# A float64 weight decoder without its sign step: Prelu with slope 2**32 in place of Copy

## The chip, the cores and the metric

The kernel runs on one core of one Trainium2 chip. The metric is device time in microseconds (us); where several executions were timed, the median is given. Engines are named as the profile names them: PE is TensorE's matrix products and PEld its weight loads, DVE is VectorE, ACT is ScalarE, POOL is GpSimd, SP is SyncE, which issues most of the DMAs.

## The reference

Linear attention over 2304 tokens is followed by two feed-forward layers (512 to 2048 to 512), the first with an ELU, the second with mish. The four weight matrices are float64. Cut to what matters:

```python
q_s = softmax(q, axis=-1)            # per head; 4 batches, 8 heads, 576 tokens, 64 wide
k_s = softmax(k, axis=2)             # over the tokens
x = einsum(q_s, einsum(k_s, v))      # 2304 tokens x 512
h = x @ w1_in                        # float64 weights
x = where(h > 0, h, exp(min(h, 0)) - 1) @ w1_out
h = x @ w2_in
return (h * tanh(log1p(exp(h)))) @ w2_out
```

## The kernel before

**The weights.** They come as the bits of their float64 values, two 32-bit words each, and are taken in pieces: one f-tile, 128 hidden units, of `w_in` or of `w_out`, 128 partitions x 512 values. There are 64 pieces, 16 f-tiles of two matrices in two layers. A piece is loaded by SP (`load_piece`), and then decoded to float32 in place:

- `rebias` (ACT, L148) rescales the high words, read as float32, by 2**-112;
- `decode_low` (DVE, L152) shifts the low words right by 29;
- `decode_sign` (DVE, L159) takes the top bit of the high word into the low word;
- `decode_join` (DVE, L166) shifts the high word left by 3 and ors the low word into it.

`piece_hi` (ACT, L186) rounds the value to its 12 leading bits, and `piece_lo` (POOL, L192) subtracts that from the value: every float32 product runs as three passes, hi*lo + lo*hi + hi*hi. Of the second layer's pieces both parts go to DRAM and come back later.

**The tokens.** The first layer takes its tokens in five blocks of four and three tiles of 128 by turns, the second in six blocks of three. In a block, a slot is one f-tile: 12 matmuls of `mm_h` (PE, L397) into one of two PSUM banks, the ELU in `elu_exp` and `elu_neg` (ACT, L405 and L409) and `elu_join` (DVE, L413, which reads the bank and so frees it), a split into hi and lo (ACT L426, DVE L430), and two slots later 12 matmuls of `mm_y` (PE, L443). Beside the products of a block run the attention steps of the next: the key chain (maximum L243, exponential L250, transposes, kv products) and the query chain (`q_max` on DVE, `q_less` L323, `q_exp` L329 on ACT, `q_sum` on DVE, `q_norm` L338, the transposes L348, `q_x` L362). In block 0 `q_less` and `q_norm` run on POOL.

**What sets the order.** Every engine takes its instructions in program order, and the program is written out by hand. Until the pipeline is full, the table `FIRST` gives the order of the steps: `1i0` is `decode_low` of piece 0 of `w_in`, `2i0` its `decode_sign`, `3i0` its `decode_join`, `b`, `p` and `l` are `rebias`, `piece_hi` and `piece_lo`; `mh` and `mr` are the two halves of a slot's `mm_h`, `ej` its `elu_join`, `gl` its low part, `my` its `mm_y`. The pieces i0 to i6 and o0 to o4 go by the table. From slot 5 of block 0 a loop does: in each slot two pieces in the rest of block 0 (`rebias` at the end of the slot ahead, `decode` behind `split_hi`, `split_piece` behind `elu_neg`), and of the second layer one piece every two slots in blocks 1 to 4.

Of the kernel before, what the change touches and what calls it, by code (L numbers as in the profile page):

```python
# [11 lines left out]
AF = mybir.ActivationFunctionType  # L12
# [5 lines left out]
EPS = 1e-9  # L18
# tanh(log1p(u)) = n / (n + 2) with n = u (u + 2). From u = 2**14 on it rounds to 1 in float32,
# as the reference's tanh does beyond its bound of 20, so u is held there.  # L20
U_MAX = 16384.0


# What comes before the pipeline is full, in the order in which the engines take it. A step's name
# tells what it does (see where they are made), and ends with the number of its pair of heads, tile
# of tokens, f-tile or piece of the weights; x0 and on are what runs beside the first slots.
FIRST = """
    km0 km1 qm0 km2 ke0 ql0 kt0 ke1 kr0 qe0 kt1 km3 ke2 kt2 qm1 kr1 ke3 ql1 ks0 ku1 qs0 kt3
    ks1 qn0 kr3 1i0 qt0 bi0 ks3 ku0 qe1 inv ku3 2i0 qm2 kv0 qs1 kr2 qm3 qn1 kv1 ku2 kv3 ql2
    kz0 ql3 ks2 qt1 qu0 kv2 kz1 qe2 qe3 3i0 kz3 kz2 qs2 qs3 qx0 qu1 1i1 pi0 qn3 qx1 bi1 bi2  # L30
    xh0 qn2 2i1 li0 xl0 qt3 qt2 xh1 qu2 1i2 xl1 qu3 qx2 xh2 2i2 3i1 1o0 qx3 xl2 xh3 pi1 bi3
    mh0 bo0 li1 xl3 mr0 1i3 mh1 mr1 3i2 bo1 2o0 pi2 ee0 en0 li2 x0 bi4 3o0 x1 ej0 2i3 1i4
    1o1 po0 2o1 ld0 gh0 bo2 3i3 ee1 mh2 gl0 mr2 2i4 lo0 en1 3i4 x2 pi3 li3 1o2 ee2 ej1 2o2
    my0 x3 en2 pi4 ld1 3o2 ej2 li4 x4 gh1 x5 mh3 gh2 x6 bo3 x7 mr3 3o1 1i5 mh4 gl1 bi5 1i6
    mr4 1o3 2i5 po1 2o3 bi6 3o3 po2 lo1 gl2 x8 ee3 x9 po3 x10 x11 2i6 ee4 3i5 my1 1o4 bo4
    en3 2o4 3i6 x12 x13 lo2 x14 pi5 3o4 ej3 lo3 en4 x15 li5 x16 ej4 gh3 my2 ld3 pi6 mh5 ld2
    mr5 po4 li6 x17 ld4 lo4 gl3 x18
""".split()
# [3 lines left out]
def attention_elu_mish(  # L42
# [10 lines left out]
):  # L53
    """The weights come as the bits of their float64 values, [..., 2] words each, low word first.

    float32 products run as three float32r passes: each operand is split exactly into
    hi (its 12 leading bits) and lo (the rest), and hi*lo + lo*hi + hi*hi accumulate in PSUM."""
    nc = tc.nc
# [8 lines left out]
    FG = NF // NG  # L67
    # The first MoE takes its tokens in blocks of four and three tiles of 128 by turns (what lies
    # on chip alternates between two buffers), the second in blocks of three.
    TILES = (4, 3, 4, 3, 4)  # L70
# [7 lines left out]
    NB = NT // TB  # L78
    # the second MoE's blocks, by tiles: the first two find theirs on chip, the others in DRAM
    back = [t for t in range(at0[NA - 2])] + [at0[NA - 1] + TPB]  # L80
# [36 lines left out]

# [1 line left out]
    # A piece is what one f-tile takes: w_in's columns, or w_out's rows, of 128 hidden units.  # L119
    raw = {}  # L120
# [22 lines left out]
    def rebias(*keys):  # L143
        # The scale moves the exponent's bias (1023 to 127, where it lies 20 bits up); three bits
        # further up it is float32's, and the sign and three more bits of the fraction go beside it.
        for key in keys:
            high = raw[key].bitcast(F32)[:, :, 1]
            nc.scalar.activation(out=high, in_=high, func=AF.Copy, scale=2.0 ** -112)  # L148

    def decode_low(*keys):  # L150
        for t in (raw[key] for key in keys):
            nc.vector.tensor_scalar(  # L152
                out=t[:, :, 0], in0=t[:, :, 0], scalar1=29, scalar2=None,
                op0=ALU.logical_shift_right,
            )

    def decode_sign(*keys):
        for t in (raw[key] for key in keys):
            nc.vector.scalar_tensor_tensor(  # L159
                out=t[:, :, 0], in0=t[:, :, 1], scalar=0x80000000, in1=t[:, :, 0],  # L160
                op0=ALU.bitwise_and, op1=ALU.bitwise_or,
            )
# [8 lines left out]
    def decode(*keys):  # L171
        decode_low(*keys)
        decode_sign(*keys)
        decode_join(*keys)
# [31 lines left out]

# [1 line left out]
    ap = att.enter_context(tc.tile_pool(name="att", bufs=2))  # L208
# [81 lines left out]
    def k_kv(b, hp, ps=None):  # L290
        e, vv = en_t.pop((b, hp)), v_t.pop((b, hp))
        if ps is None:
            ps = att_psum()
        for c in range(NC):
            n = min(P, S - c * P)
            # a head's half of the array's columns is all that it needs, and both work at once
            for a in (0, D):
                nc.tensor.matmul(  # L298
                    out=ps[a:a + D, a:a + D], lhsT=e[0:n, c, a:a + D], rhs=vv[0:n, c, a:a + D],
                    start=(c == 0), stop=(c == NC - 1),  # L300
                )
        kv_t[b, hp] = ps
# [80 lines left out]

# [1 line left out]
    h_t, e_t, gh_t, gl_t, y_t = {}, {}, {}, {}, {}  # L385
# [62 lines left out]
    def end_y(j):  # L448
        for e in range(KD):
            ps = y_t[e][:, 0:TILES[j] * P]  # L450
            hi, lo = xh[j][:, e, :], xl[j][:, e, :]
            nc.scalar.activation(out=hi, in_=ps, func=AF.Copy)
            nc.vector.tensor_tensor(out=lo, in0=ps, in1=hi.bitcast(F32), op=ALU.subtract)
        # tiles that lie side by side on either side go together
        runs = []
        for t in range(at0[j], at0[j] + TILES[j]):
            if t in back:
                b, o = divmod(back.index(t), TPB)
                if runs and runs[-1][0] == b and o:
                    runs[-1][3] += 1  # L460
                else:
                    runs.append([b, o, t - at0[j], 1])
        for b, o, t, n in runs:
            for d, x in zip(x2_d[b], (xh[j], xl[j])):
                nc.gpsimd.dma_start(
                    out=d[:, :, o * P:(o + n) * P], in_=x[:, :, t * P:(t + n) * P]
                )

    # mish(h) = h n / (n + 2) with u = e**h, n = u (u + 2). The reciprocal is e**-ln(n + 2), which
    # one step of Newton's method makes exact to float32. What two f-tiles need goes turn by turn.  # L470
    def mish(f, old, older):
# [66 lines left out]
    x2 = {}  # L538
# [5 lines left out]

    # the second batch's values are loaded early, where the second block's tokens will lie
    for n, t in enumerate(("xhb", "xlb")):
        t = xpool.tile([P, KD * TB], F32, tag=t, name="early_x")
        for hp in (2 * n, 2 * n + 1):
            a = hp % 2 * NC * P
            v_t[1, hp] = t[:, a:a + NC * P].rearrange("p (c e) -> p c e", e=P)  # L550
# [1 line left out]
    beside = {}  # L552
# [9 lines left out]
    def kv_chain(j, f, b):  # L562
        for hp in range(NHP):
            # the slots in which a load is emitted lie behind what frees its buffer
            s = f + 2 * hp
# [25 lines left out]

    # the first layer's pieces come in the first block's slots, two in each
    turns = {-1: [("i", 0, 0), ("i", 0, 1)]}
# [8 lines left out]
    for j in range(NA - 1):  # L602
        if j + 1 < B:
            kv_chain(j, 0, j + 1)
        for o in range(TILES[j + 1]):
            q_chain(j, (8 if TILES[j + 1] == TPB else 6) + 2 * o, at0[j + 1] + o)
    # the second MoE's are decoded over the other blocks, and wait in DRAM
    for n in range(NF):
# [10 lines left out]
    with tc.manual_schedule():  # L619
        nc.scalar.preload_act_table_set("natural_log_exp_and_others")  # L620
        two = const.tile([P, 1], F32, name="two")
        nc.vector.memset(two, 2.0)
        # what comes first is loaded at once, where later weights will lie
        tags = ("wih", "wil", "woh", "wol")
# [54 lines left out]
        for hp in range(2, NHP):  # L679
            load_v(1, hp, v_t[1, hp])  # L680
        # the array's clock rises only once the array has been busy
        warm = ps_h.tile([P, 512], F32, tag="h", name="t")
# [15 lines left out]
        def step(name, fn, *a):  # L698
            first[name] = lambda: fn(*a)
# [22 lines left out]
        for key in [key for f in range(-1, AHEAD) for key in turns[f]]:  # L722
            n = f"{key[0]}{key[2]}"
            step("b" + n, rebias, key)
            step("1" + n, decode_low, key)
            step("2" + n, decode_sign, key)
            step("3" + n, decode_join, key)
            step("p" + n, piece_hi, *key)
            step("l" + n, piece_lo, *key)
        # the first products take their tokens by halves  # L730
        half = slice(0, 2 * P), slice(2 * P, 4 * P)
# [55 lines left out]
        for s in range(len(slots) + LAG2):  # L787
            if s < len(slots):
                p, f = slots[s]
                # two banks that the second block's outputs take lend room while the pipe fills  # L790
                mm_h(1, *x2[p], f, TB, pool=(ps_a, "a") if p == 0 and f in (2, 3) else None)
# [47 lines left out]
```

## Time and profile before

| | |
|---|---|
| median of 3 runs | 886.6 us (885.91 to 886.83) |
| profiled execution, its span from first to last instruction | 885.3 us |
| what lies around the span, as the difference of the two | 1.3 us |
| PE, DVE, ACT, POOL busy | 866.6, 643.9, 471.9, 168.1 us |
| last sign step of VectorE | in block 4 of the first layer, before 470 us |

The time of the profiled execution beside its span is not given by itself; the median of the runs stands for it. Busy shares are averages over stages that have different limits. The stages here are the attention of the first block (to 27 us), the fill of the pipeline (to 59 us), the rest of block 0 (to 125.5 us), blocks 1 to 4 of the first layer (to 470 us), and the second layer. A PE that is busy in a stage sets its pace; where PE is idle, what it waited for is looked up. The clock column is the granted TensorE clock as a share of full speed.

### The profile page before, as it was taken

The page shows a single profiled execution, that of the slowest core. Times are in us where ns is not written, and L with a number is a line of the kernel's source. Part 1 is how long each engine was busy: PE and PEld are TensorE (multiplying, and loading weights), DVE is VectorE, ACT ScalarE, POOL GpSimd, SP SyncE. Part 2 cuts the span into 40 slices and gives each one's busy share as a digit, 9 for nine tenths or more (in the row PEclk, how much of TensorE's full clock was granted, in tenths as well). Part 3 has the DMA queues.
Part 4 walks back from the last instruction along what each step waited for, and adds up shares of the span by engine and source line. Part 5 has one row for each costly group of instructions (what it writes and reads, how often), then busy time and mean ns, then how long its engine had stood idle before and what let it go on. Part 6 is the DMA issues. An engine that isn't in the chain of part 4 may idle for free.

```text
span 885.3 us, 12486 instructions
## 1 busy us (share of the span) xinstructions
PE 866.6 (98%) x4644; PEld 769.7 (87%) x4644; DVE 643.9 (73%) x1210; ACT 471.9 (53%) x935; POOL 168.1 (19%) x183
## 2 busy tenths in 40 slices
PE   8889999999999999999999999999999999999998
PEld 5878779999888899998888899999999999999996
DVE  7999976776555557845444977778877877877875
ACT  6768756655655455554444544444544544544443
POOL 2346653322321233223333000000000000000000
PEclk7999999999999999999999999999999999999999
DMA  9763364654634355536977302102002102000100
GB/s 299 235 195 128 118 211 117 197 176 141 170 107 147 96 162 152 163 96 191 284 243 224 129 1 72 37 0 72 37 1 72 37 1 72 36 1 1 37 1 36
DMA packets 60381, 99.37 MB, mean 112 GB/s; under 512 B 4001, under 2 KB 38817, under 8 KB 58273
## 3 DMA queue, kind: packets, MB, share of 16 engines
q1 hardware_dynamic: 38720, 52.44, 19.4%
q0 software_dynamic: 21600, 46.14, 17.0%
q8 instruction: 36, 0.59, 0.3%
q14 instruction: 25, 0.20, 0.1%
HBM read 70.78 MB, written 27.79 MB: 111 GB/s over the span
## 4 chain that ended last, share of the span: by engine, by line
PE 85%; DVE 9%; issue 3%; ACT 1%; DMA 1%; POOL 0%; SPq 0%; POOLq 0%; DVEq 0%; ACTq 0%
PE h L397 40%; PE y L443 19%; PE y L523 15%; PE a L523 7%; DVE early L159 2%; DVE early L166 2%; PE a L362 1%; DVE early L152 1%; DVE gl L430 1%; DVE e L413 1%; PE a L348 1%; PE a L298 1%; PE t L298 1%; DMA early<-in_kT_dram 1%; DVE raw L159 0%
## 5 line engine op out<-in xcount | busy, mean ns | idle before, releaser
L397 PE MATMUL h<-xha,wil 128*128 128x384 f32 (+2 forms) x408 | 144.6, 354 | 4.1 <-DVE ks L254 2.8
L397 PE MATMUL h<-xha,wih 128*128 128x384 f32 (+2 forms) x408 | 144.5, 354 | 0.0
L397 PE MATMUL h<-xla,wih 128*128 128x384 f32 (+2 forms) x408 | 144.2, 353 | 0.0
L495 ACT ACTIVATE r<-n,two 128x384 f32<-128x384 f32 x96 | 59.5, 619 | 132.1 <-DVE n L491 132.1
L443 PE MATMUL y<-gh,wol 128*128 128x512 f32 (+1 forms) x320 | 122.8, 384 | 0.0
L443 PE MATMUL y<-gl,woh 128*128 128x512 f32 (+1 forms) x320 | 118.3, 370 | 0.5 <-DVE gl L430 0.5
L443 PE MATMUL y<-gh,woh 128*128 128x512 f32 (+1 forms) x320 | 118.4, 370 | 0.0
L413 DVE SCALAR_TENSOR_TENSOR e<-h,e 128x512 f32<-128x512 f32 (+1 forms) x80 | 50.8, 636 | 89.1 <-ACT e L409 89.0
L397 PE MATMUL h<-xhb,wih 128*128 128x384 f32 x320 | 107.6, 336 | 0.0
L397 PE MATMUL h<-xhb,wil 128*128 128x384 f32 x320 | 107.4, 336 | 0.0
L397 PE MATMUL h<-xlb,wih 128*128 128x384 f32 x320 | 107.3, 335 | 0.0
L405 ACT ACTIVATE e<-h 128x512 f32<-128x512 f32 (+1 forms) x80 | 44.3, 554 | 108.6 <-PE h L397 108.6
L192 POOL TENSOR_TENSOR lo<-raw,hi 128x512 fp32r<-128x512 f32 x32 | 45.9, 1435 | 240.0 <-ACT hi L186 147.6
L397 PEld LDWEIGHTS h<-xha,wil 128*128 128x128 f32 x408 | 77.3, 190 | 13.9 <-issue 5.0
L474 ACT ACTIVATE u<-h 128x384 f32<-128x384 f32 x96 | 47.1, 491 | 74.7 <-PE h L397 74.7
L397 PEld LDWEIGHTS h<-xla,wih 128*128 128x128 f32 x408 | 77.3, 189 | 8.6
L484 DVE TENSOR_SCALAR u<-u 128x384 f32<-128x384 f32 x96 | 35.3, 368 | 66.5 <-ACT u L474 66.5
L397 PEld LDWEIGHTS h<-xha,wih 128*128 128x128 f32 x408 | 77.3, 189 | 6.5
L523 PE MATMUL y<-woh,gl 128*128 128x512 f32 x192 | 76.1, 397 | 0.0
L523 PE MATMUL y<-woh,gh 128*128 128x512 f32 x192 | 76.0, 396 | 0.0
L523 PE MATMUL y<-wol,gh 128*128 128x512 f32 x192 | 74.7, 389 | 0.0
L430 DVE TENSOR_TENSOR gl<-e,gh 128x512 fp32r<-128x512 f32 (+1 forms) x80 | 51.7, 646 | 29.3 <-ACT gh L426 29.3
(139 smaller groups left out, 1820.0 us busy)
## 6 DMA issues: line engine op xcount, KB each, us to landing
raw<-in_moe_w_out_dram SPq DMA_DIRECT2D x23, 512.0 KB, 4.3
raw<-in_moe_w_in_dram SPq DMA_DIRECT2D x21, 512.0 KB, 5.1
early<-in_moe_w_in_dram SPq DMA_DIRECT2D x11, 512.0 KB, 6.0
early<-in_moe_w_out_dram SPq DMA_DIRECT2D x9, 512.0 KB, 6.2
out_dram<-o SPq DMA_DIRECT2D x18, 256.0 KB, 2.3
q<-in_q_dram SPq DMA_DIRECT2D x16, 256.0 KB, 5.1
w2ih<-hi POOLq DMA_DIRECT2D x16, 256.0 KB, 3.9
w2il<-lo POOLq DMA_DIRECT2D x16, 256.0 KB, 4.9
```

Of the source, the lines that this page charges most:

```text
L159: nc.vector.scalar_tensor_tensor(out=t[:, :, 0], in0=t[:, :, 1], scalar=0x80000000, in1=t[:, :, 0], op0=ALU.bitwise_and, op1=ALU.bitwise_or,)
L166: nc.vector.scalar_tensor_tensor(out=t[:, :, 1], in0=t[:, :, 1], scalar=3, in1=t[:, :, 0], op0=ALU.logical_shift_left, op1=ALU.bitwise_or,)
L192: nc.gpsimd.tensor_tensor(out=lo, in0=z, in1=hi.bitcast(F32), op=ALU.subtract)
L397: nc.tensor.matmul(out=h_t[f][:, c], lhsT=w[:, i, k * P:(k + 1) * P], rhs=x[:, k, c], start=(n == 0), stop=(n == 3 * KD - 1),)
L405: nc.scalar.activation(out=e, in_=h_t[f], func=AF.Exp)
L413: nc.vector.scalar_tensor_tensor(out=e, in0=h_t[f], scalar=0.0, in1=e, op0=ALU.max, op1=ALU.subtract)
L430: nc.vector.tensor_tensor(out=gl_t[f], in0=h_t.pop(f), in1=gh_t[f].bitcast(F32), op=ALU.subtract)
L443: nc.tensor.matmul(out=y_t[e][:, 0:gh.shape[1]], lhsT=w[:, i, e * P:(e + 1) * P], rhs=x, start=(f == 0 and n == 0), stop=(f == NF - 1 and ...
L474: nc.scalar.activation(out=u, in_=h_t[f], func=AF.Exp)
L484: nc.vector.tensor_scalar(out=u, in0=u, scalar1=U_MAX, scalar2=None, op0=ALU.min)
L495: nc.scalar.activation(out=r, in_=n, func=AF.Ln, bias=two)
L523: nc.tensor.matmul(out=y_t[p, t], lhsT=x[:, c], rhs=w[:, i, :], start=(f == 0 and n == 0), stop=(f == NF - 1 and n == 2),)
```

## The change

`rebias` uses the function Prelu in place of Copy: with the scale of 2**-112 and a slope of 2**32 on the negative side. A negative word then has an exponent that is 32 higher, and the bit for 32 in it is the one that the shift by 3 in `decode_join` brings to the place of the sign. `decode_sign` goes, and with it its steps in `FIRST`; the join, which was step 3, is now step 2. The other steps stand in the order that they had.

```diff
         for key in keys:
             high = raw[key].bitcast(F32)[:, :, 1]
-            nc.scalar.activation(out=high, in_=high, func=AF.Copy, scale=2.0 ** -112)
+            nc.scalar.activation(
+                out=high, in_=high, func=AF.Prelu, scale=2.0 ** -112, alpha=2.0 ** 32
+            )
...
-    def decode_sign(*keys):
-        for t in (raw[key] for key in keys):
-            nc.vector.scalar_tensor_tensor(
-                out=t[:, :, 0], in0=t[:, :, 1], scalar=0x80000000, in1=t[:, :, 0],
-                op0=ALU.bitwise_and, op1=ALU.bitwise_or,
-            )
-
...
     def decode(*keys):
         decode_low(*keys)
-        decode_sign(*keys)
         decode_join(*keys)
...
-            step("2" + n, decode_sign, key)
-            step("3" + n, decode_join, key)
+            step("2" + n, decode_join, key)
```

Of the table one line shows the pattern:

```diff
-    mr4 1o3 2i5 po1 2o3 bi6 3o3 po2 lo1 gl2 x8 ee3 x9 po3 x10 x11 2i6 ee4 3i5 my1 1o4 bo4
+    mr4 1o3 po1 bi6 2o3 po2 lo1 gl2 x8 ee3 x9 po3 x10 x11 ee4 2i5 my1 1o4 bo4
```

The lines below `decode_sign` move up by five in the changed kernel: `decode_low` is L155 there, `decode_join` L162, `elu_join` L408, the low part L425.

On VectorE at the end of the fill, from the low part of f-tile 1 to the ELU join of f-tile 3 (`early_134` and `early_135` hold raw pieces), there stands before:

```order
L430 TENSOR_TENSOR gl_596<-e_473,gh_546 128x512
L152 TENSOR_SCALAR early_135<-early_135 128x512
L152 TENSOR_SCALAR early_134<-early_134 128x512
L159 SCALAR_TENSOR_TENSOR early_134<-early_134 128x512 x2
L166 SCALAR_TENSOR_TENSOR early_134<-early_134 128x512
L430 TENSOR_TENSOR gl_620<-e_514,gh_562 128x512
L159 SCALAR_TENSOR_TENSOR early_135<-early_135 128x512
L166 SCALAR_TENSOR_TENSOR early_134<-early_134 128x512
L152 TENSOR_SCALAR early_135<-early_135 128x512
L159 SCALAR_TENSOR_TENSOR early_135<-early_135 128x512
L166 SCALAR_TENSOR_TENSOR early_135<-early_135 128x512 x2
L413 SCALAR_TENSOR_TENSOR e_624<-h_549,e_624 128x512
```

And in the changed kernel, at the same place on VectorE:

```order
L425 TENSOR_TENSOR gl_588<-e_467,gh_538 128x512
L155 TENSOR_SCALAR early_135<-early_135 128x512
L155 TENSOR_SCALAR early_134<-early_134 128x512
L162 SCALAR_TENSOR_TENSOR early_134<-early_134 128x512
L425 TENSOR_TENSOR gl_610<-e_507,gh_554 128x512
L162 SCALAR_TENSOR_TENSOR early_134<-early_134 128x512
L155 TENSOR_SCALAR early_135<-early_135 128x512
L162 SCALAR_TENSOR_TENSOR early_135<-early_135 128x512 x2
L408 SCALAR_TENSOR_TENSOR e_614<-h_541,e_614 128x512
```

The four sign steps (L159) between the two are gone; what is left stands in the order of before.

On VectorE in the later slots of block 0, two slots with their query chain (`qs` and `qm` are its sums and maxima), there stands before:

```order
L152 TENSOR_SCALAR raw<-raw 128x512 x2
L159 SCALAR_TENSOR_TENSOR raw<-raw 128x512 x2
L166 SCALAR_TENSOR_TENSOR raw<-raw 128x512 x2
L430 TENSOR_TENSOR gl<-e,gh 128x512
L413 SCALAR_TENSOR_TENSOR e<-h,e 128x512
L382 TENSOR_TENSOR xlb<-a,xhb 128x4x128
L333 TENSOR_REDUCE qs<-q 128x8
```

And in the changed kernel:

```order
L155 TENSOR_SCALAR raw<-raw 128x512 x2
L162 SCALAR_TENSOR_TENSOR raw<-raw 128x512 x2
L425 TENSOR_TENSOR gl<-e,gh 128x512
L408 SCALAR_TENSOR_TENSOR e<-h,e 128x512
L377 TENSOR_TENSOR xlb<-a,xhb 128x4x128
L328 TENSOR_REDUCE qs<-q 128x8
```

The two sign steps ahead of the low part, the ELU join and the query sums are gone. The instructions of PE, ACT, POOL and SP stand as before; on ACT the function of the 64 rescalings is another, and one load of a function table stands ahead of them all in both kernels.

## Rows read from the trace of the kernel before

**Rows 1.** The page's head: span, and busy time of each engine.

```profile
span 885.3 us, 12486 instructions
PE 866.6 (98%) x4644; PEld 769.7 (87%) x4644; DVE 643.9 (73%) x1210; ACT 471.9 (53%) x935; POOL 168.1 (19%) x183
```

**Rows 2.** Stretches of the span: busy time by engine, clock, DMA share.

```profile
core 0: us, PE busy (x) PEld busy (x) DVE busy (x) ACT busy (x) POOL busy (x), PEclk, DMA share, GB/s
...
27.10:59.13 32.03, 26.54 (x189) 22.87 (x188) 31.72 (x44) 22.04 (x43) 13.75 (x9) 1.00 0.59 183
59.13:125.50 66.37, 63.46 (x344) 52.40 (x345) 62.63 (x98) 48.85 (x90) 40.45 (x26) 0.95 0.46 148
125.50:470.00 344.50, 343.61 (x1910) 307.15 (x1909) 208.63 (x349) 186.68 (x359) 95.80 (x119) 1.00 0.57 168
```

**Rows 3.** TensorE's waits over the span: us in total, times, longest us.

```profile
PE h L397 <- DVE ks L254: 2.8, 1, 2.8
PE a L348 <- POOL q L338: 2.8, 2, 1.9
...
PE h L397 <- DVE e L413: 1.2, 2, 0.8
```

**Rows 4.** Short stretches, columns as in rows 2: the clock behind two pauses.

```profile
59.10:61.00 1.90, 1.86 (x14) 1.90 (x15) 1.90 (x4) 1.90 (x4) 0.70 (x1) 0.87 0.91 276
61.00:63.40 2.40, 2.40 (x12) 2.21 (x11) 2.40 (x2) 2.21 (x5) 2.33 (x2) 0.50 0.74 250
63.40:65.00 1.60, 1.60 (x26) 1.44 (x25) 1.60 (x4) 1.23 (x2) 0.00 (x0) 0.84 1.11 296
...
118.50:120.00 1.50, 1.50 (x6) 1.40 (x7) 1.50 (x4) 0.52 (x1) 0.00 (x0) 0.51 0.82 283
120.00:123.50 3.50, 3.50 (x13) 2.75 (x12) 3.40 (x6) 2.34 (x4) 2.16 (x2) 0.72 0.26 102
```

**Rows 5.** Stretches, the sign step's line L159 alone: VectorE busy (count).

```profile
0.00:27.10 27.10, 2.67 (x3) 0.75 0.99 309
27.10:59.13 32.03, 8.31 (x9) 1.00 0.59 183
59.13:125.50 66.37, 16.96 (x19) 0.95 0.46 148
125.50:470.00 344.50, 33.00 (x33) 1.00 0.57 168
```

**Rows 6.** Timeline of VectorE at the end of the fill: start, us, instruction.

```profile
52.54 0.69 DVE L159 SCALAR_TENSOR_TENSOR early<-early 128x512 uint32<-128x512 uint32 x1
53.14 1.81 DVE L166 SCALAR_TENSOR_TENSOR early<-early 128x512 uint32<-128x512 uint32 x1
...
58.31 0.68 DVE L413 SCALAR_TENSOR_TENSOR e<-h,e 128x512 f32<-128x512 f32 x1
```

**Rows 7.** Timelines of GpSimd and VectorE near the end of block 0.

```profile
94.19 1.91 POOL L192 TENSOR_TENSOR wol<-raw,woh 128x512 fp32r<-128x512 f32 x1
...
108.41 4.91 POOL L192 TENSOR_TENSOR wol<-raw,woh 128x512 fp32r<-128x512 f32 x1
...
109.05 1.28 DVE L159 SCALAR_TENSOR_TENSOR raw<-raw 128x512 uint32<-128x512 uint32 x2
```

**Rows 8.** ScalarE's groups by form over the span: busy us, mean ns.

```profile
L409 ACT ACTIVATE e<-e 128x512 f32<-128x512 f32 x48 | 30.3, 632 | 1.4
...
L148 ACT ACTIVATE early<-early 128x512 f32<-128x512 f32 x20 | 12.7, 677 | 0.7 <-DMA early<-in_moe_w_in_dram 0.7
L329 ACT ACTIVATE q<-q 128x512 f32<-128x512 f32 x16 | 9.9, 618 | 3.3 <-POOL q L323 3.3
...
L620 ACT ACT_TABLE_LOAD x1 | 1.3, 1283 | 0.7 <-PEq L822 0.7
```

**Rows 9.** Timeline of TensorE, two transposes with the wait ahead of each.

```profile
104.02 0.66 PE L348 MATMUL a<-ident,q 128*128 128x128 f32 x4 [0.82 <-POOL q L338]
...
118.47 1.10 PE L348 MATMUL a<-ident,q 128*128 128x128 f32 x4 [1.94 <-POOL q L338]
```

More of the change, by code (lines that the diff above doesn't have):

```diff
@@ L27 @@
 FIRST = """
[L28 to L34, printed above, removed]
-    mr4 1o3 2i5 po1 2o3 bi6 3o3 po2 lo1 gl2 x8 ee3 x9 po3 x10 x11 2i6 ee4 3i5 my1 1o4 bo4
-    en3 2o4 3i6 x12 x13 lo2 x14 pi5 3o4 ej3 lo3 en4 x15 li5 x16 ej4 gh3 my2 ld3 pi6 mh5 ld2
-    mr5 po4 li6 x17 ld4 lo4 gl3 x18
+    km0 km1 qm0 km2 ke0 ql0 kt0 ke1 kr0 qe0 kt1 km3 ke2 kt2 qm1 kr1 ke3 ql1 ks0 ku1 qs0 kt3 ks1 qn0
+    kr3 1i0 qt0 bi0 ks3 ku0 qe1 inv ku3 qm2 kv0 qs1 kr2 qm3 qn1 kv1 ku2 kv3 ql2 kz0 ql3 ks2 qt1 qu0
+    kv2 kz1 qe2 qe3 2i0 kz3 kz2 qs2 qs3 qx0 qu1 1i1 pi0 qn3 qx1 bi1 bi2 xh0 qn2 li0 xl0 qt3 qt2 xh1
+    qu2 1i2 xl1 qu3 qx2 xh2 2i1 1o0 qx3 xl2 xh3 pi1 bi3 mh0 bo0 li1 xl3 mr0 1i3 mh1 mr1 2i2 bo1 pi2
+    ee0 en0 li2 x0 bi4 2o0 x1 ej0 1i4 1o1 po0 ld0 gh0 bo2 2i3 ee1 mh2 gl0 mr2 lo0 en1 2i4 x2 pi3 li3
+    1o2 ee2 ej1 my0 x3 en2 pi4 ld1 2o2 ej2 li4 x4 gh1 x5 mh3 gh2 x6 bo3 x7 mr3 2o1 1i5 mh4 gl1 bi5
+    1i6 mr4 1o3 po1 bi6 2o3 po2 lo1 gl2 x8 ee3 x9 po3 x10 x11 ee4 2i5 my1 1o4 bo4 en3 2i6 x12 x13
+    lo2 x14 pi5 2o4 ej3 lo3 en4 x15 li5 x16 ej4 gh3 my2 ld3 pi6 mh5 ld2 mr5 po4 li6 x17 ld4 lo4 gl3
+    x18
 """.split()
```

## The prediction

> **What bounds the kernel now.** I read the head of the page first. TensorE is busy for 866.6 of 885.3 us [rows 1], so nearly all of the time is matmul work that the change doesn't touch. The sign steps run on VectorE, which is busy for 643.9 us; what they cost shows only where TensorE stands idle. So I next cut the span into stretches [rows 2]. The reader is to see that from 27.10 to 59.13 us, while the pipeline fills, VectorE is busy for 31.72 of 32.03 us and TensorE for only 26.54; that from 59.13 to 125.50, the rest of the first block, VectorE is still busy for 62.63 of 66.37 us and TensorE short by 2.91; and that from 125.50 to 470.00 TensorE lacks only 0.89 of 344.50 us. There, and in the second MoE, which decodes no weights, a shorter VectorE gives nothing. Third, the list of what TensorE waited for [rows 3]: 2.8 us in one wait for VectorE at the end of the fill (it is put down to a small step on ks; what frees the bank is the ELU join just ahead of it), 1.2 us for two ELU joins, 2.8 us in two waits for a GpSimd step of the query chain. Last, the granted clock [rows 4]: it is 1.00, which is 2.4 GHz, over the fill [rows 2] although TensorE pauses there for up to 0.8 us [rows 3], and falls to 0.50 and 0.51, the level of 1.2 GHz, behind the two longest pauses, 2.8 us [rows 3] and 1.94 us [rows 9]. Everything that the change can win lies between 27 and 126 us.
>
> **What a sign step costs on VectorE.** There are 64: 3 before 27.10 us, 9 in the fill, 19 in the rest of block 0, 33 later [rows 5]. The first three I cost at nothing: what starts the first product at 27.1 us is TensorE's own attention work and ScalarE's copies of its results. Busy time of the nine in the fill is 8.31 us, 0.92 each, but that isn't the saving. One that meets no GpSimd work lasts 0.69 us, and the next instruction starts 0.60 us after it: the sign step at 52.54 and the join at 53.14 [rows 6]. The rest of the 8.31 us is standing still while a GpSimd subtraction runs; the nine subtractions remain, and the join behind will stand instead. So I take 0.60 us each: 9 x 0.60 = 5.4 us in the fill; the ends are 0.60 and 0.92 each, 5.4 and 8.3 us.
>
> The row that shows this exclusion from the other side: at 108.41 a GpSimd subtraction lasts 4.91 us where one at 94.19 lasts 1.91, and beside the long one VectorE runs two signs in 1.28 us, undisturbed [rows 7]. The Trainium skill, "SBUF — State Buffer", section "Who interferes with whom", says that a VectorE instruction with two inputs in SBUF and a GpSimd instruction that reads SBUF exclude each other for the whole instruction. By that rule 5.4 us is the saving, and by plain busy time it would be 8.3; the rows agree with the rule.
>
> **What ScalarE's new function costs.** No row shows Prelu. The nearest rows are the rescaling as it is now, a Copy of 128x512 with stride two at 0.677 us, and other functions on tiles of that size: Exp 0.618, Relu 0.632 [rows 8]. Those two differ by 0.014 us, so I take Prelu at 0.677 like the Copy that it replaces, with the same operands; the bounds are -0.06 and +0.06 us each, at most 0.7 us over the twelve of the fill even were all of them on the path. The join now bears the wait for ScalarE that the sign step had; it stands at its old place, so nothing is queued longer behind it.
>
> **The sum.** First the fill. TensorE's idle time in it is 32.03 - 26.54 = 5.49 us. Without it the product that now starts at 59.13 would start at 27.10 + 26.54 = 53.6. VectorE's own chain says when it could: the ELU join which it waits for starts at 58.31 [rows 6]; less 5.4 that is 52.9, and it takes 0.68 us, so its reader starts at about 53.7. The two ends meet within 0.1 us: VectorE gives up the lead and TensorE takes it. I take 5.0 of 5.49, half a microsecond for a subtraction that now falls in a worse place. Second, the clock. Behind the 2.8 us pause the stretches show 0.87 over 1.9 us, 0.50 over 2.4 and 0.84 over 1.6 [rows 4]: 0.25 + 1.20 + 0.26 = 1.7 us lost. If no such pause is left it comes back; I take 1.4. Third, the query chain. TensorE's transposes at 104.02 and 118.47 wait 0.82 and 1.94 us for GpSimd's normalising step [rows 9], which waits for VectorE's sums. A slot of this stretch decodes two pieces, so VectorE gets there 2 x 0.60 = 1.2 us earlier in each slot, and over ten slots its lag behind TensorE vanishes. That covers the 0.82. The 1.94 comes from the subtraction of 4.91 us: of what it stood behind (two shifts, two signs, two joins, one subtraction) the two signs go, 1.2 us, and VectorE itself comes 1.2 us earlier, 2.4 in all. I take 0.8 + 1.6 = 2.4. Fourth, the clock behind that pause: 0.51 over 1.5 us and 0.72 over 3.5 [rows 4], 0.74 + 0.98 = 1.7 us; I take 1.3. Sum: 5.0 + 1.4 + 2.4 + 1.3 = 10.1 us. The 33 later signs give nothing: TensorE covers them.
>
> Against the profiled execution: 885.3 - 10.1 = 875.2 us. The median is 886.6 us, 1.3 above that span, so the forecast is **876.5 us**. If every pause and every slow stretch went, 5.49 + 1.7 + 2.76 + 1.7 = 11.7 us, it would be 874.9. What is late next is TensorE itself, whose work has not shrunk. The weights' loads wait for buffers that GpSimd's subtractions free, and these come no later than now; the transfers have room at shares of 0.59 and 0.46 [rows 2].
>
> **The rivals.** *ScalarE takes over the fill.* It is busy for 22.04 of 32.03 us there [rows 2], and takes everything in one fixed order, so a copy of high parts that waits for a join holds up the next exponential. For it: the copies follow joins closely. Against it: with a third of its time idle it can give back more than the 5.4 us. If half the fill's pause stays, 2.5 us are lost, and with the pause its slow clock, 1.4: a gain of 6.2, 880.4 us. *GpSimd keeps the late pauses.* It doesn't get shorter, and which engine gets in first is chance as 1.91 against 4.91 us shows. If both waits and the clock behind them stay, 3.7 us are lost: 880.2 us. Both together: 884.1 us.
>
> *Slower: table loads.* If the set of functions that is active doesn't hold Prelu, each group of rescalings takes one load to it and one back. A load is 1.283 us, and before there is one in the whole program [rows 8]. The fill has six such groups: 6 x 2.57 = 15.4 us on ScalarE, 22.04 + 15.4 = 37.4 against 32.03, 5.4 us late. The rest of the block has about ten: 48.85 + 25.7 = 74.5 against 66.37, 8.2 us late. 886.6 + 13.6 = 900 us. In the rest of the block ScalarE has 66.37 - 48.85 = 17.5 us to spare, so it decides there from the seventh such pair of loads on, and in the fill, with 10 us to spare, from the fourth. Against it: the built program of the changed kernel has a single load, at the same place. The Trainium skill, "ScalarE: Activation LUTs", section "Table sets: the hidden batching unit", names relu, copy, identity and abs as present in every set, and not Prelu; with its figure of about 2.66 us per switch the same two stretches would lose some 58 us, an estimate from that page. No row here shows which.
>
> *No gain.* The join takes over the sign step's stalls at full length, and new ones come at worse places, so that VectorE ends the fill where it did: 886 us. Against it are nine instructions fewer on an engine that is full.
>
> **How the numbers follow.** The forecast has 0.72, ScalarE in the fill 0.08, GpSimd's late pauses 0.11, both 0.03, no gain 0.03, table loads 0.03. The forecast's own ends are 874.9 (all pauses gone) and 878.5 (2 us of new stalls). The range reaches up to the two middle rivals and a little beyond, and down to a bound under the sum for the ends of the sign step and Prelu: 874.3 to 881.5. It leaves out both together, no gain and table loads, and some of the edges. A measurement of this kernel can tell about 0.2%, 1.8 us, from no change: faster by more than that are the forecast and the next three, 0.94; within it no gain, 0.03; slower 0.03.
>
> **What would show it.** In the profile of the changed kernel TensorE's busy time from 27 us to the sixth f-tile's product should have no wait over 1 us, and that product should start at about 53 to 54 us; the clock should be 1.00 from 27 us through 130; the waits for GpSimd's normalising step should be gone or under half a microsecond; the rescaling should last 0.68 us; and the second MoE should last as long as before. The prediction is wrong if ScalarE shows more than one table load, if the fill ends at 57 us or later with VectorE still full, or if a wait of two microseconds for GpSimd stands near 110 us.

## The result, and the profile after

The changed kernel takes 871.5 us (median of 4 runs, 871.08 to 873.06) against 886.25 us (4 runs, 884.60 to 886.83) of the kernel before: a ratio of 0.9843, interval 0.9831 to 0.9856, 14.75 us less. The forecast was 876.5, its range 874.3 to 881.5. Two later comparisons of the same two kernels gave 12.75 us less (0.9854, interval 0.9832 to 0.9876) and 12.47 us less (0.9860, interval 0.9841 to 0.9879). So direction and places were right, and the size was too small.

The head of the page of the changed kernel, which answers to [rows 1]:

```profile
span 870.1 us, 12421 instructions
PE 858.6 (99%) x4644; PEld 764.6 (88%) x4644; DVE 600.8 (69%) x1146; ACT 470.3 (54%) x935; POOL 162.3 (19%) x183
```

VectorE is busy 43.1 us less, not the 60.9 us that the 64 sign steps took [rows 5]: a part of each lay beside the next instruction, which starts 0.60 us after a step of 0.69 [rows 6], and a part was standing still, some of which now stands elsewhere. All that TensorE waited for in the changed kernel (total us, times, longest), to be read beside [rows 3]:

```profile
PE t L260 <- ACT early L245: 3.2, 2, 3.0
PE t L679 <- DVE two L617: 1.5, 1, 1.5
PE a L357 <- ACT early L347: 1.2, 1, 1.2
PE a L343 <- ACT kT L265: 0.7, 1, 0.7
PE a L357 <- ACT kvbd L303: 0.4, 1, 0.4
```

The wait at the end of the fill, the two ELU joins and the two waits for GpSimd are gone; of the five that are left, four stand ahead of the first product. The stretches of the changed kernel, cut at the first product, at those of the sixth and seventh f-tile, and at two later slots (columns as in [rows 2]):

```profile
25.02:50.50 25.48, 25.39 (x189) 23.07 (x188) 23.38 (x36) 22.66 (x45) 13.58 (x9) 1.00 0.68 221
50.50:57.60 7.10, 7.10 (x61) 6.33 (x61) 4.56 (x8) 5.17 (x10) 3.21 (x3) 1.00 1.06 379
57.60:82.70 25.10, 25.10 (x147) 20.20 (x146) 23.27 (x36) 21.66 (x44) 15.22 (x12) 1.00 0.32 114
82.70:108.50 25.80, 25.73 (x130) 21.43 (x129) 22.81 (x33) 19.23 (x35) 14.99 (x13) 1.00 0.60 185
```

Of the kernel before, the fill is in [rows 2]; the three stretches behind it, cut at the same products:

```profile
59.13:67.80 8.67, 8.66 (x61) 7.80 (x62) 8.67 (x13) 7.30 (x15) 4.28 (x3) 0.80 0.89 275
67.80:93.10 25.30, 25.16 (x148) 20.22 (x147) 25.15 (x41) 19.63 (x38) 13.80 (x11) 1.00 0.26 93
93.10:123.30 30.20, 27.44 (x129) 22.56 (x128) 26.65 (x45) 21.29 (x39) 21.32 (x14) 0.94 0.50 159
```

By the starts of these products, in us:

| stretch | before | changed | less |
|---|---|---|---|
| head, to the first product | 27.11 | 25.02 | 2.09 |
| fill, to the sixth f-tile's product | 32.02 | 25.53 | 6.49 |
| to the seventh f-tile's product | 8.64 | 7.07 | 1.57 |
| to the last slots of block 0 | 55.56 | 50.85 | 4.71 |
| the rest, to the end of the span | 762.0 | 761.6 | 0.4 |

The sum is 15.2 us, the difference of the two spans. The changed kernel's profiled execution took 871.89 us, 1.8 more than its span; with the same 1.8, an estimate, the profiled execution of the kernel before took 887.1, slower than any that was timed beside the changed kernel. So some of the 15.2 us can be chance in that one execution. I had given the fill 5.0, the clock behind it 1.4, the query chain and its clock 3.7, and the head nothing. The experiments ask three things: whether the head's 2 us are the change's, why the fill gave more, and what in block 0 is the sign step's.

### The profile page after: what moved, and what is told of

It is laid out like the page before. It is cut to its first block, busy times and chain, and to the rows that moved or that the text cites. A ratio compares the mean times of both kernels' runs of the same rounds, so it can differ in the third digit from the quotient of the medians.

```text
span 870.1 us, 12421 instructions
## 1 busy us (share of the span) xinstructions
PE 858.6 (99%) x4644; PEld 764.6 (88%) x4644; DVE 600.8 (69%) x1146; ACT 470.3 (54%) x935; POOL 162.3 (19%) x183
## 4 chain that ended last, share of the span: by engine, by line
PE 96%; DMA 1%; ACT 1%; POOL 0%; issue 0%; DVE 0%; SPq 0%; POOLq 0%; ACTq 0%
PE h L392 46%; PE y L438 23%; PE y L518 15%; PE a L518 8%; PE a L357 2%; PE a L293 1%; PE a L343 1%; PE a L260 1%; DMA early<-in_q_dram 1%; DMA early<-in_kT_dram 1%; POOL early L318 0%; PE a L274 0%; SPq L216 0%; ACT kvbd L303 0%; ACT e L400 0%
## 5 line engine op out<-in xcount | busy, mean ns | idle before, releaser
L408 DVE SCALAR_TENSOR_TENSOR e<-h,e 128x512 f32<-128x512 f32 (+1 forms) x80 | 50.9, 636 | 112.6 <-ACT e L404 112.2
L425 DVE TENSOR_TENSOR gl<-e,gh 128x512 fp32r<-128x512 f32 (+1 forms) x80 | 52.4, 655 | 31.7 <-ACT gh L421 31.5
```

The costliest lines, as they stand in the source:

```text
L408: nc.vector.scalar_tensor_tensor(out=e, in0=h_t[f], scalar=0.0, in1=e, op0=ALU.max, op1=ALU.subtract)
L425: nc.vector.tensor_tensor(out=gl_t[f], in0=h_t.pop(f), in1=gh_t[f].bitcast(F32), op=ALU.subtract)
```

## The experiments

Every kernel was profiled and timed beside the kernel before in the same session. Stretches are those of the table; "head 25.0, fill 25.5" means their lengths. What the kernel before gave in those sessions is 884.44, 885.42 and 885.05 us.

### The sign step dropped in the fill only

```diff
+    def signed(kind, layer, f):
+        table = layer == 0 and f < (7 if kind == "i" else 5)
+        return not table
...
-            nc.scalar.activation(out=high, in_=high, func=AF.Copy, scale=2.0 ** -112)
+            if signed(*key):
+                nc.scalar.activation(out=high, in_=high, func=AF.Copy, scale=2.0 ** -112)
+            else:
+                nc.scalar.activation(
+                    out=high, in_=high, func=AF.Prelu, scale=2.0 ** -112, alpha=2.0 ** 32
+                )
...
-        for t in (raw[key] for key in keys):
+        for t in (raw[key] for key in keys if signed(*key)):
```

> The sign step is dropped (Prelu) only for the twelve pieces whose order the table gives, i0 to i6 and o0 to o4; the other 52 keep Copy and the sign step. Theory A (the gain has two separate places, the end of the fill and the query chain at the end of block 0, and what the head of the program gained is no effect of the change): the sixth f-tile's product starts 5 to 6 us earlier, the clock stays at 1.00 behind it, and the gain is 7 to 8 us of the 14.75; the waits of 0.8 and 1.9 us for GpSimd near 104 and 118 us stay. Theory B (VectorE is the pace of all of block 0, one long chain): the gain of the fill is partly lost again in the slots behind it, under 5 us stay. If the head's 2 us belong to the first three sign steps they come on top: 9 to 10 us.

Measured: 878.8 us, 5.6 less than before (ratio 0.9933, interval 0.9915 to 0.9951). Head 25.0, fill 25.49, next 7.08: all as in the changed kernel. But the last stretch takes 57.34 us where the kernel before takes 55.56. TensorE's waits for GpSimd's normalising step there are three instead of two, and GpSimd shows the long subtraction again:

```profile
PE a L357 <- POOL q L347: 4.6, 3, 1.9
...
100.02 4.89 POOL L201 TENSOR_TENSOR wol<-raw,woh 128x512 fp32r<-128x512 f32 x1
```

So the gain of the fill is 6.5 us and the clock 1.6, and 1.8 us of it are lost again in block 0, nearly all in the third wait, of 1.8 us at 81.4. The gain lies between what theory A and theory B said. Theory A's places hold; theory B is right in that a VectorE full of sign steps doesn't keep all of an earlier start.

### The sign step dropped everywhere but in the fill

```diff
-        return not table
+        return table
```

> The other way round: the twelve pieces of the table keep Copy and the sign step, the other 52 lose it. Theory A: the fill ends as before (the sixth f-tile's product at about 59 us behind a pause of 2.8 us, the clock falls), the two waits for GpSimd near the end of block 0 go, with the slow clock behind the second: a gain of 4 to 5 us. Theory B: VectorE, relieved only later, has nothing to give back: under 2 us.

Measured: 879.47 us, 5.0 less (ratio 0.9948, interval 0.9929 to 0.9968). The fill is that of before, 31.99 us, with its pause; block 0 takes 50.85 us, exactly as in the changed kernel. The wait at the end of the fill, and the stretch behind it:

```profile
PE h L406 <- DVE ks L263: 2.8, 1, 2.8
...
58.40:68.20 9.80, 9.80 (x60) 8.96 (x61) 9.27 (x13) 8.36 (x17) 5.43 (x4) 0.69 0.85 274
```

The two places are separate, as theory A has it: what block 0 gains comes from its own sign steps. Behind the same pause of 2.8 us the clock cost more here, 9.83 us against 8.64.

### The sign step dropped for i0, i1 and i2 only

```diff
-        return not table
+        return not (layer == 0 and kind == "i" and f < 3)
```

> Only i0, i1 and i2 lose the sign step, the three whose sign step stands ahead of the first product. Theory A: the first product starts when it did (25 to 27 us, as the clock of the first 25 us falls out), no change in the median, within 1 us. Rival: the 2.1 us that the first product came earlier in the changed kernel are the effect of these three: a gain of about 2 us, and the profile shows full clock from about 16 us on.

Measured: 884.6 us, ratio 1.000 (interval 0.9986 to 1.0014). The first product starts at 26.18 us; fill and next are 31.99 and 8.64. The three sign steps ahead of the first product are worth nothing, as predicted, and the rival falls.

Block 0 has all its sign steps here, and takes 53.91 us, 1.6 less than in the kernel before. TensorE waits there as it did [rows 9], but behind the longest of these pauses the clock doesn't fall. First the 5 us behind it in the kernel before, then the pause and the 5 us behind it here (the clock is the third value from the end):

```profile
118.50:123.50 5.00, 5.00 (x17) 4.16 (x18) 4.90 (x9) 2.86 (x5) 2.16 (x2) 0.66 0.43 156
```

```profile
117.47 0.65 PE L357 MATMUL a<-ident,q 128*128 128x128 f32 x4 [1.95 <-POOL q L347]
...
117.50:122.50 5.00, 5.00 (x24) 4.22 (x25) 4.90 (x9) 3.48 (x7) 2.20 (x2) 1.00 0.48 152
```

So of the 4.7 us of block 0 in the table some 3.1 are the waits, and 1.6 are a slow clock that kernels with all of these sign steps show in some profiles and not in others.

### Prelu with slope 1, all sign steps kept

```diff
-            nc.scalar.activation(out=high, in_=high, func=AF.Copy, scale=2.0 ** -112)
+            nc.scalar.activation(
+                out=high, in_=high, func=AF.Prelu, scale=2.0 ** -112, alpha=1.0
+            )
```

> All 64 rescalings use Prelu, with slope 1, and all sign steps stay: the function is changed and nothing else. If Prelu costs what Copy costs, the rescaling lasts 0.67 to 0.68 us and the time is that of the kernel before, within 1 us. If Prelu were cheaper or dearer than Copy, the rescaling's mean would move, and the time with it by up to 64 times the difference.

Measured: 885.11 us, ratio 1.0008 (interval 0.9995 to 1.0020). The rescaling and the one table load, as groups of ScalarE (busy us, mean ns):

```profile
L152 ACT ACTIVATE raw<-raw 128x512 f32<-128x512 f32 x44 | 29.2, 674 | 1.0 <-DMA raw<-in_moe_w_out_dram 0.8
L152 ACT ACTIVATE early<-early 128x512 f32<-128x512 f32 x20 | 12.8, 686 | 0.6 <-DMA early<-in_moe_w_in_dram 0.5
L626 ACT ACT_TABLE_LOAD x1 | 1.3, 1283 | 0.7 <-PEq L828 0.7
```

Prelu costs what Copy costs [rows 8], and there is no second load. Block 0 takes 53.96 us, at a clock of 1.00 behind the same pause of 1.9 us, as in the run before this one. This run also shows what the head is: all its sign steps are there, and yet its first product starts at 25.27 us. The stretch from 16 to 20 us of the kernel before, the changed one, this one, and the changed one once more (the clock is the third value from the end):

```profile
16.00:20.00 4.00, 4.00 (x48) 3.17 (x44) 3.89 (x8) 2.60 (x7) 1.42 (x1) 0.50 1.04 374
```

```profile
16.00:20.00 4.00, 3.58 (x53) 2.85 (x50) 3.86 (x9) 3.70 (x10) 1.27 (x1) 1.00 1.05 377
```

```profile
16.00:20.00 4.00, 3.72 (x50) 2.99 (x46) 3.86 (x10) 3.42 (x8) 0.92 (x1) 1.00 1.08 383
```

```profile
16.00:20.00 4.00, 4.00 (x47) 3.17 (x44) 3.86 (x10) 2.39 (x6) 1.20 (x1) 0.50 1.05 371
```

The clock in the head is at the lower or the higher of its two levels from one execution to the next, with sign steps and without, and the first product follows it.

### The changed kernel again

> The changed kernel once more, beside the kernel before on one chip in one session. The 14.75 us of the first comparison hold, by theory A, about 13 us that belong to the change (6.5 in the fill, 1.6 by the clock behind it, 4.5 in the query chain and the clock behind that, 0.3 later) and up to 2 us of a clock that rises earlier or later in the first 25 us whatever the kernel: 12 to 13.5 us here. Rival: all 14.75 belong to the change: 14 to 15.5 us, and the first product stands at 25 us in the changed kernel and at 27 in the kernel before in most executions.

Measured: 872.67 us, 12.75 less (0.9854, interval 0.9832 to 0.9876). In the profiled execution the first product starts at 26.53 us, at the slow clock shown last above, and the other stretches are 25.51, 7.07 and 50.86 us, within 0.02 of the first profile. The change's stretches repeat; its head does not.

### The sign step kept in the second layer only

```diff
-        return not table
+        return layer == 1
```

> Only the 32 pieces of the second layer, decoded in blocks 1 to 4, keep Copy and the sign step; the first layer's 32 lose it. If TensorE covers VectorE from 126 us on, the time is that of the changed kernel, within 0.5 us. Rival: the 0.3 us that the changed kernel gained between 310 and 346 us, and sign steps there, count: 0.5 to 1.5 us slower than the changed kernel.

Measured: 873.67 us, 1.0 above the changed kernel beside it, with ratios to the kernel before of 0.9870 (0.9854 to 0.9886) and 0.9854 (0.9832 to 0.9876) that overlap: not told apart. The spans differ by 0.5 us, of which 0.4 lie in the head. VectorE's sign steps and joins of blocks 2 to 4 here, and the joins of the changed kernel in the same stretch, 200 to 480 us:

```profile
L168 DVE SCALAR_TENSOR_TENSOR raw<-raw 128x512 uint32<-128x512 uint32 x24 | 26.5, 1104 | 6.1 <-ACT raw L153 4.5
...
L175 DVE SCALAR_TENSOR_TENSOR raw<-raw 128x512 uint32<-128x512 uint32 x24 | 16.6, 694 | 0.8
```

```profile
L162 DVE SCALAR_TENSOR_TENSOR raw<-raw 128x512 uint32<-128x512 uint32 x24 | 25.4, 1060 | 6.1 <-ACT raw L149 4.5
```

Here nearly all of the standing still does move to the join, as I had it: the sign step stands 0.41 us beyond its 0.69, and without it the join goes from 694 to 1060 ns. And it costs TensorE next to nothing.

### Every sign step twice

```diff
-        for t in (raw[key] for key in keys):
+        for t in (raw[key] for key in keys if signed(*key) for n in range(2)):
```

> The kernel before with every sign step done twice (the second sets the bit that is set). VectorE bounds the fill and block 0: nine more in the fill at 0.60 to 0.92 us, 5.4 to 8.3 us later, and in block 0 a VectorE that is 94 percent busy gets 1.2 to 1.8 us more in each of ten slots: 12 to 18 us. Together 16 to 26 us slower than the kernel before, more than the change gains, since nothing covers it; the sign steps of blocks 1 to 4 cost nothing. Rival: pauses are set by single waits and not by VectorE's sum: the loss is as the gain, 10 to 13 us.

Measured: 905.8 us, 20.4 more than before (ratio 1.0234, interval 1.0215 to 1.0252), within what was expected. Fill 37.99 us, 5.97 more for nine sign steps: 0.66 us each. Block 0 takes 65.65, 10.1 more than in the kernel before, less than the 12 to 18 that were expected of it. The rest, from the end of block 0 on, takes 1.5 us more, where nothing was expected. TensorE's longest waits:

```profile
PE a L357 <- POOL q L347: 9.7, 3, 4.6
PE h L406 <- DVE ks L263: 4.7, 2, 4.0
```

With the steps doubled VectorE's sum is the pace of the fill and of most of block 0; the rival, a loss as large as the gain, falls.

### The sign step kept for o0 to o4

```diff
-        return not table
+        return table and kind == "o"
```

> As the changed kernel, but o0 to o4, five of the nine pieces whose sign step lies in the fill, keep Copy and the sign step. In the kernel before the stretch from the first product to that of the sixth f-tile lasts 32.0 us, in the changed one 25.5. If VectorE's sum is the pace until TensorE's own 25.5 us are reached, four sign steps fewer at 0.67 to 0.92 us make it 28.3 to 29.3 us, and the time is 3 to 5 us above the changed kernel's. Rival: a few single waits set the fill, and some of the nine steps count more than others: 26 to 27 us or above 30.

Measured: 877.05 us, 4.5 above the changed kernel beside it. The fill takes 28.70 us, inside 28.3 to 29.3, so four sign steps fewer are worth 3.3 us, 0.83 each. TensorE waits again:

```profile
PE h L406 <- POOL wil L201: 1.6, 1, 1.6
...
PE h L406 <- DVE e L422: 0.8, 1, 0.8
```

With five more gone the fill would be 24.5 us at that rate and 25.4 at the 0.66 of the doubled steps; it is 25.5, and TensorE has no wait left there. So in the changed kernel TensorE bounds the fill, and VectorE, busy for 23.38 of 25.48 us, has some time over.

### Products of zeros in the pause of the head

```diff
+        def warm_more():
+            t = ps_h.tile([P, 512], F32, tag="h", name="t")
+            z = kvbd[0].rearrange("p c e -> p (c e)")
+            for n in (512, 256):
+                nc.tensor.matmul(
+                    out=t[:, 0:n], lhsT=kvbd[0][:, 0, :], rhs=z[:, 0:n], start=True, stop=True
+                )
+
+        step("wm", warm_more)
```

with `wm` behind `kt1` in the table; first in the changed kernel, then in the kernel before, then in the changed kernel again beside it.

> The changed kernel with two more products of zeros, 512 and 256 columns wide, in TensorE's pause of 2 to 3 us near 7 us, so that no long pause stands in front of the kv products. Theory: the clock of 0.50 from about 9.5 us to 13, 15 or 21 us is the sequel of that pause; without it the clock stays at 1.00, the first product starts at 23.5 to 25 us in each execution, the spread of the times shrinks, and the median is 0.5 to 2 us below the changed kernel. Rival: the clock falls all the same, or the chain through ScalarE and VectorE bounds the head: no change, or up to 0.5 us slower.

> The kernel before with the two products of zeros in TensorE's pause near 7 us and nothing else. If the clock of the first 25 us is independent of the sign steps, the first product starts near 25 us at full clock as it does with the same products in the changed kernel, the rest of the program is moved as a whole, and the median is 0.5 to 1.5 us below the kernel before, with a smaller spread. Rival: with the sign steps in it the head is bound by VectorE: no gain.

> The changed kernel a third time, beside the next one: 12 to 14 us below the kernel before, a spread of some 2 us, and in the profiled run the first product between 25 and 27 us as the clock of the head falls out.

> The changed kernel with the two products of zeros once more, beside the changed kernel on the same chip: the median 0.5 to 1.5 us below it and a spread of 1 us or less, the first product at 24.8 us. Rival: no difference between the two medians.

Measured: the changed kernel with them 871.58 us beside 872.67 without, and 872.51 beside 872.58. The clock does what the theory said; in all three profiles with these products it is 1.00 throughout the head (here the first of them), and the first product starts at 24.76 to 25.03 us:

```profile
10.00:13.00 3.00, 1.76 (x23) 1.28 (x25) 2.11 (x7) 2.49 (x8) 0.51 (x1) 1.00 1.13 331
```

But the medians don't part, against what was expected, and the spread of the second series is not smaller, 871.57 to 874.19. In the third profile of the changed kernel, without them, the first product starts at 24.77 as well. So no version beats the changed kernel, and what spreads its times by 2 us is not settled.

The kernel before with them gains nothing either, where 0.5 to 1.5 us were expected: 886.22 us, ratio 1.0008 (interval 0.9997 to 1.0020). Its profile shows where a better head can go. The head is 25.03, the fill 31.91, the next stretch only 7.15, and block 0 takes 57.02 us with three waits for GpSimd and the long subtraction:

```profile
PE a L348 <- POOL q L338: 4.4, 3, 1.9
...
106.19 4.92 POOL L192 TENSOR_TENSOR wol<-raw,woh 128x512 fp32r<-128x512 f32 x1
```

The 2.1 us of the head and 1.5 of the clock behind the fill are seen in the profile and not in the median: 1.5 of the 3.6 go in block 0 of that execution, and for the rest one profile doesn't speak for twelve runs.

## Why the prediction was wrong

**What bounds the kernel: right.** All of the change's gain but 0.4 us lies between the first product and the end of block 0. The removal in each place alone, and the doubling, show VectorE as its cause. Alone the two places give 5.6 and 5.0 us, together 12.5 and more: what the first gains is kept in full only when the second is relieved too.

**The price of Prelu and the table loads: right.** In the changed kernel the rescaling and the load stand as in [rows 8], so the slower rival has no ground:

```profile
L149 ACT ACTIVATE early<-early 128x512 f32<-128x512 f32 x20 | 12.9, 688 | 2.1 <-DMA early<-in_moe_w_in_dram 1.3 <-DMA early<-in_moe_w_out_dram 0.8
L615 ACT ACT_TABLE_LOAD x1 | 1.3, 1283 | 0.7 <-PEq L816 0.7
```

**The first term of the sum failed: the fill, 5.0 us by the prediction, 6.5 by the runs.** Both ends that were to meet at 53.6 us were wrong. The first is VectorE's: "the nine subtractions remain, and the join behind will stand instead". VectorE's groups in the fill, first of the kernel before, then of the changed one (busy us, mean ns):

```profile
L166 DVE SCALAR_TENSOR_TENSOR early<-early 128x512 uint32<-128x512 uint32 x11 | 12.6, 1156 | 0.1
L159 DVE SCALAR_TENSOR_TENSOR early<-early 128x512 uint32<-128x512 uint32 x9 | 8.3, 932 | 0.1
L152 DVE TENSOR_SCALAR early<-early 128x512 uint32<-128x512 uint32 x9 | 5.8, 669 | 0.0
...
L430 DVE TENSOR_TENSOR gl<-e,gh 128x512 fp32r<-128x512 f32 x3 | 2.1, 684 | 0.0
```

```profile
L162 DVE SCALAR_TENSOR_TENSOR early<-early 128x512 uint32<-128x512 uint32 x10 | 10.6, 1067 | 0.1
L425 DVE TENSOR_TENSOR gl<-e,gh 128x512 fp32r<-128x512 f32 x4 | 4.6, 1140 | 0.5 <-ACT gh L421 0.5
L408 DVE SCALAR_TENSOR_TENSOR e<-h,e 128x512 f32<-128x512 f32 x5 | 3.4, 683 | 1.2 <-ACT e L404 1.2
L155 DVE TENSOR_SCALAR early<-early 128x512 uint32<-128x512 uint32 x8 | 3.2, 421 | 0.0
```

Take an undisturbed join, sign or low part at 0.69 us and a shift at 0.42. Before, standing still is 5.0 us in joins, 2.1 in signs, 2.0 in shifts, none in low parts: 9.1 us for nine GpSimd subtractions. After, it is 3.7 in joins, 1.8 in low parts and none in shifts: 5.5 us for nine. So only part of it moved, and 3.6 us went. Instruction by instruction, each of the nine subtractions before holds one instruction of VectorE, a join, a sign or a shift, to between 1.49 and 1.82 us. In the changed kernel six do, to between 1.35 and 1.82 us. The three that start at 29.48, 37.39 and 48.64 us hold none: beside them VectorE stands idle for ScalarE, or runs an ELU join, a key maximum or small steps, which keep their lengths. One of the three, and what VectorE runs beside it:

```profile
48.64 1.32 POOL L187 TENSOR_TENSOR wil<-early,wih 128x512 fp32r<-128x512 f32 x1 [3.09 <-ACT wih L181]
...
49.12 0.69 DVE L408 SCALAR_TENSOR_TENSOR e<-h,e 128x512 f32<-128x512 f32 x1 [0.62 <-ACT e L404]
```

VectorE's busy time of the fill fell from 31.7 to 23.4 us, 8.3 less. That is the upper end of what I had worked out, where I took the lower, but the agreement is in part luck: cut at TensorE's products the two windows hold 44 and 36 instructions of VectorE, and not the same ones but for nine sign steps. The rule of the Trainium skill that I leaned on ("SBUF — State Buffer", section "Who interferes with whom") isn't against this: it says who excludes whom, and not that a stall must find a new victim. In blocks 2 to 4 nearly all of the stall did move.

The second end is TensorE's floor. I read 26.54 us of work out of the busy column [rows 2] and took the other 5.49 for all that there was to win. The changed kernel does the same 189 matmuls in 25.48 us. A busy record is longer than the distance to the next matmul, and where a pause follows, the whole record is counted: a product of 256 columns is shown at 0.28 us and one follows another every 0.12. From the kernel before, with a pause of the fill, which is shown as 0.79 us and is 0.95 beyond the 0.12:

```profile
33.04 0.28 PE L397 MATMUL h<-xla,wih 128*128 128x256 f32 x1
33.16 0.28 PE L397 MATMUL h<-xha,wih 128*128 128x256 f32 x1
34.23 0.36 PE L397 MATMUL h<-xha,wil 128*128 128x256 f32 x1 [0.79 <-DVE e L413]
```

Six such pauses hide about 1 us of idle time. The upper bound of 11.7 us, and the lower end of the range with it, rested on that column; they were no bounds, as the fill alone gave 6.49 us where they allowed 5.49.

**The clock behind the fill: right in kind.** 1.57 us came back, of 1.4 taken and 1.7 at most. The price of the same pause is not constant, though: 9.83, 8.64 and 7.15 us for the stretch behind 2.8 us of idle time.

**The query chain and its clock: 4.7 us in the two profiles, where I took 3.7.** I had left 0.3 of the 1.94 and 0.4 of the clock behind; all of it came back, and the slots ahead are 0.2 us shorter. The mechanism of the waits was right: no GpSimd subtraction of that stretch is longer than 1.6 us in the changed kernel, no wait for its normalising step is left, and the one that took 4.91 us [rows 7] takes 1.50:

```profile
96.08 1.50 POOL L187 TENSOR_TENSOR wol<-raw,woh 128x512 fp32r<-128x512 f32 x1
```

The term for the clock, 1.3 us, was no fixed price. In three profiles with these sign steps the clock falls behind the pause of 1.9 us, and in two, with Prelu in three pieces and with Prelu at slope 1, it doesn't. Measured against those two the place gives 3.1 us, less than I took. So the fill, shorter by 6.4 to 6.5 us against every profile that has its sign steps, is the term that was surely too small.

**The head: 2.1 us that are not the change's.** I had it at nothing, and the run that drops only its sign steps, and the one that keeps them all, agree. It is in the two profiles and chance there; the later comparisons, at 12.75 and 12.47 us, are nearer to the 13 us of the other stretches, of which 1.6 are the clock in block 0. The lower end of my range lies 12.3 us under the kernel before, and the 11.7 us of my upper bound lie inside the intervals of both. But both give more than the 10.1 of the forecast, and their intervals, from 10.7 us on, leave that out: chance can account for some 2 us of the first comparison, and not for the fill.

The rivals got too much room on the cautious side. ScalarE's roundings of the first pieces waited 6.4 us for joins of VectorE before and 0.5 us in the changed kernel, and GpSimd's late waits went once the sign steps of block 0 were gone.

## What to carry to other kernels

A busy column is no floor for an engine that pauses: count the distance from one matmul to the next, or add to the idle time the tail of the last record ahead of each pause. Where two engines exclude each other, price a removed instruction from both sides, its undisturbed time and its whole busy time, and let the range reach to the upper one if the engine will have pauses afterwards. An engine that is full can lose an earlier start again a few stages on, here 1.5 to 1.8 us of it in block 0; to keep it, relieve the later stage too. One profile of each kernel is one draw of the clock behind each pause: compare the stretch over several runs before a term gets a price from it.

## What the runs showed of the hardware

The same GpSimd subtraction, the 26th of the 32, lasted 4.89 to 4.92 us in all five kernels that have the sign steps of block 0 once, at five places in time from 100.0 to 108.4 us. Without them it lasted 1.50 to 1.51 us, and with every step twice no subtraction lasted over 1.93. So its length comes with the order of the instructions and was not the chance that I had called it, but a VectorE that runs back to back isn't enough for it; what is, stays open. Another, the seventh, lasted 3.0 us in three of the five kernels that have all sign steps of the fill once, and 1.5 us in the other two, so chance has a part there.

The clock after a pause is not the pause's alone: after 2.8 us of idle time the stretch of 7.07 us at full clock took 7.15, 8.64 and 9.83 us in three kernels with the same instructions on TensorE between the first product and the pause. After 1.9 us of idle time near the end of block 0 it was 0.66 over the next 5 us in three kernels and 1.00 in two. In the head the same program showed 0.50 and 1.00 in the same 4 us in two executions.
